# Five token blocks instead of seven in the first layer of an attention and feed-forward kernel

## The chip, the cores and the metric

The kernel runs on one core of a Trainium2 chip. Its metric is the device time of one execution in microseconds (us); the number told for a kernel is the median of its runs.

## What is computed

Attention over 4 batches, 8 heads, 576 positions and a head dimension of 64, with a mask that lets a position see 32 earlier ones: the last 32 for heads 0 to 3, and every fourth of the last 128 ("dilated") for heads 4 to 7. Its result, 2304 tokens of 512 features, goes through two layers with 2048 hidden features.

```python
scores = scale * np.matmul(q, k.transpose(0, 1, 3, 2))
scores = np.where(masks[None, :, :, :], scores, -1000000000.0)
attn = exp(scores - max) ; attn = attn / (attn.sum + 1e-09)
x = (attn @ v) as 2304 x 512
x = (h - tanh(h)) @ w_out,            h = x @ w_in       # layer one
out = (h * sigmoid(h)) @ w_out2,      h = x @ w_in2      # layer two
```

## The kernel before

**Features lie on the partitions.** `X` holds x^T: 4 groups of 128 features, each twice (a leading part in the short format `F32R`, and the rest, "hi" and "lo"), with 1152 columns, which is two batches of 576 tokens used in turn. Each product of the layers is made of three passes of TensorE (`passes`, L541): lo with hi, hi with hi, hi with lo.

**The layers run in token blocks.** `FIRST` lists those of layer one (seven, of 512, 304, 336, 272, 304, 272 and 304 tokens), and layer two has 4 of 512 and one of 256. In a block, 16 slots `f` each take 128 hidden features: `h` in 12 passes (4 feature groups of 3), the gate (tanh on ScalarE, a product or difference on VectorE, hi on ScalarE, lo on VectorE), and then the 12 passes of `y` for an earlier slot: one slot behind with blocks of more than `WIDE` tokens and in layer two, two behind with the small ones. Accumulators of `h` have two banks and those of `y` four.

**Weights are prepared on the chip.** A chunk (one slot of w_in or w_out) is loaded to a stage and goes through ScalarE three times (`prelu` L160, `lows` L165, `leading` L127), VectorE twice (`shift` L170, `trailing` L183) and GpSimd once (`join` L174). Layer one has 32 chunks. Those of layer two (`Feed`) are taken into the weight tiles of layer one while its last blocks still run: `FEED2` says how many chunks a slot takes, by `f % 3`.

**Attention runs in pairs of heads**, 16 of them. Batch 0 is done before layer one can start, by units of 192 positions: masked scores on TensorE, a maximum on VectorE, three exponentials on ScalarE, a division, a transpose on TensorE, the product with v, and the results into `X`. Batch 1 lies between the passes of block 0. All of that, with the weights of layer one and block 0 itself, is put in order by `play`, a planner with a cost for each step and due times (`SLOT0`, `SLOT`, `DUE`, `NEXT0`, `NEXT`); each engine executes its list strictly in that order.

**Batches 2 and 3 lie between the slots of the later blocks**, by numbered ticks. `STARTS` gives the tick at which a pair begins, and `plan` its steps: transposes of q and k on VectorE, scores, masks, exponentials, the division, eight transposes of the probabilities on VectorE, the product with v. `ORDER` is the order of the steps of a slot: gate `g`, hi `G`, lo `L`, `Y` the passes of y, `t` one tick, `F` the weights of layer two.

`WARM` products at the very start have no result that is used.

Of the kernel before, what the change touches and what calls it, by code (L numbers as in the profile page):

```python
# [8 lines left out]
F32 = mybir.dt.float32  # L9
F32R = mybir.dt.float32r  # L10
# [15 lines left out]
DIL = 4  # L26
MASKED = -1e30
# [4 lines left out]
def tile_kernel(  # L32
# [59 lines left out]

    def play(ops, free):
# [4 lines left out]
        while todo:  # L98
# [11 lines left out]
            t, o = min((x for x in first[e] if x[0] <= t + NEAR), key=lambda x: x[1].rank)  # L110
            o.fn(ENGINE[e])
# [21 lines left out]
    class Chunk:  # L133


        def __init__(self, store, key, src, is_in):
            self.store, self.key, self.src, self.is_in = store, key, src, is_in

# [137 lines left out]
    nc.scalar.copy(out=mask[QB:], in_=half)  # L276
    mask_dil = [mask[:, UB * u:UB * (u + 1)] for u in range(NU)]
    mask_plain = [mask[:, 0::5]] + [mask[:, NB - 1:]] * (NU - 1)

    kT1 = cpool.tile([P, S], F32, name="kT")  # L280
# [4 lines left out]
    class Pair:  # L285
# [220 lines left out]
        def values(self, n0, n1, pool=None, tag="o"):  # L506
# [5 lines left out]
            x = X[:, :, :, S * (self.b % 2):S * (self.b % 2 + 1)]  # L512
            src = o.rearrange("p m c -> p (m c)")
            s0, s1 = QB * n0, QB * n1
            if self.dil:
                dst = [x[:, w, self.c, s0:s1] for w in range(2)]
            else:
                i0, i1 = s0 // DIL, s1 // DIL
                dst = [x[:, w, self.c, :].rearrange("p (r i) -> p i r", r=DIL)[:, i0:i1, :] for w in range(2)]
                src = src.rearrange("p (i r) -> p i r", r=DIL)  # L520
            self.left[n0] = dst, src

        def x_hi(self, engine, n0):
            dst, src = self.left[n0]
            copy(engine, dst[0], src)

        def x_lo(self, n0):
            dst, src = self.left.pop(n0)
            nc.vector.tensor_tensor(out=dst[1], in0=src, in1=dst[0].bitcast(F32), op=ALU.subtract)
# [13 lines left out]
    class First:  # L543


        def __init__(self, t0, n):
            self.t0, self.n, self.layer = t0, n, 0
            self.x = X[:, :, :, t0 % (2 * S):t0 % (2 * S) + n]

        def parts(self, c):  # L550
            return [self.x[:, a, c] for a in range(2)]

# [4 lines left out]
        def begin(self, f, c, h):  # L557
# [4 lines left out]
            passes(h, [w[:, a, c, :] for a in range(2)], self.parts(c), c == 0, c == NC - 1)  # L562
            return h

        def second(self, f, g, opool):
            for c in range(NC):
                self.second_part(f, c, g)
            if f == NF - 1:
                for a, dst in ((0, y1_hi), (1, y1_lo)):
                    nc.sync.dma_start(out=dst[:, :, self.t0:self.t0 + self.n].rearrange("c p t -> p c t"),  # L570
                                      in_=self.x[:, a].bitcast(F32))

        def second_part(self, f, c, g):
            w = wout[0, f]
            if c == 0 and f == 0:
                self.y = [ps_y.tile([P, 512], F32, tag=f"y{k}", name=f"y{k}")[:, :self.n] for k in range(NC)]
            if True:
                passes(self.y[c], [w[:, a, c * P:(c + 1) * P] for a in range(2)],
                       [g[:, a] for a in range(2)], f == 0, f == NF - 1)
                if f == NF - 1:  # L580
                    hi, lo = self.parts(c)
                    nc.scalar.activation(out=hi, in_=self.y[c], func=AF.Copy)
# [426 lines left out]
```

## Time and profile before

| | |
|---|---|
| time, median of 3 runs | 915.97 us (915.05 to 916.33) |
| profiled execution | 915.71 us, of which the span in the profile is 913.9 us |
| TensorE busy | 896.9 us (98%) |
| VectorE, ScalarE, GpSimd busy | 436.0, 398.0, 122.6 us |
| mean granted TensorE clock | 0.986 of full |

The span is the time from the first to the last instruction. A share that is an average over the span says little here, since the start, the later part of layer one and layer two have different limits.

### The profile page before, as it was taken

To read this page: it belongs to the slowest core of one execution; us is meant where nothing else is said; L and a number is where in the kernel's file an instruction comes from. 1 tells how busy PE (TensorE), PEld (TensorE's weight loads), DVE (VectorE), ACT (ScalarE), POOL (GpSimd) and SP (SyncE) were. 2 spreads that over 40 slices of the span, in tenths; PEclk is the share of its full clock that TensorE was granted. 3 is DMA by queue.
4 is the path that set the end of the run, shared out by engine and by line. 5 is a ranking of instruction groups with operands and counts; after the bars stand their busy time and mean duration, and the time that the engine had idled before them with its cause. 6 is when DMAs were issued, how large, how long until landed. Compare 5 with 4: busy or idle time off the path is not lost.

```text
span 913.9 us, 15235 instructions
## 1 busy us (share of the span) xinstructions
PE 896.9 (98%) x5998; PEld 782.8 (86%) x5998; DVE 436.0 (48%) x836; ACT 398.0 (44%) x969; POOL 122.6 (13%) x164
## 2 busy tenths in 40 slices
PE   7999999999999999999999999999999999999997
PEld 5677778999999999999999888888888888888896
DVE  2468887446756666433266666422222222222232
ACT  5689875334443334423266666432223222322322
POOL 8333553000010000000022222100000000000000
PEclk9599999999999999999999999999999999999999
DMA  9966335213223322024044564140004000200100
GB/s 232 281 153 167 98 96 117 93 28 82 49 50 58 97 35 69 20 70 147 1 141 139 186 214 139 46 136 3 1 1 139 0 1 1 93 0 1 32 15 24
DMA packets 122375, 74.39 MB, mean 81 GB/s; under 512 B 84896, under 2 KB 110528, under 8 KB 122304
## 3 DMA queue, kind: packets, MB, share of 16 engines
q1 hardware_dynamic: 121472, 72.57, 28.6%
q0 software_dynamic: 832, 0.85, 0.4%
q8 instruction: 47, 0.77, 0.4%
q14 instruction: 24, 0.20, 0.1%
HBM read 59.24 MB, written 14.16 MB: 80 GB/s over the span
## 4 chain that ended last, share of the span: by engine, by line
PE 85%; DVE 5%; ACT 4%; issue 2%; DMA 2%; SPq 2%; DVEq 0%; ACTq 0%
PE h L541 39%; PE y L541 39%; PE s L432 3%; PE o L510 2%; DMA st<-in_moe_w_in_dram 1%; ACT w L127 1%; ACT st L160 1%; DVE g L555 1%; DVE pT L492 1%; SPq L359 1%; PE y L432 1%; PE h L387 1%; ACT gg L969 1%; DVE w L183 1%; DVE st L170 1%
## 5 line engine op out<-in xcount | busy, mean ns | idle before, releaser
L541 PE MATMUL h<-x,w 128*128 128x512 f32 (+4 forms) x2304 | 439.5, 338 | 0.8
L541 PEld LDWEIGHTS h<-x,w 128*128 128x128 f32 x2304 | 365.6, 188 | 45.2 <-DVE g L555 2.5
L541 PE MATMUL y<-gg,w 128*128 128x304 f32 (+3 forms) x1344 | 226.8, 314 | 0.0
L541 PE MATMUL y<-w,gg 128*128 128x512 f32 x864 | 209.8, 390 | 0.4 <-ACT gg L969 0.4
L541 PEld LDWEIGHTS y<-gg,w 128*128 128x128 f32 x1344 | 197.6, 188 | 8.8 <-DVE gg L882 0.7
L541 PEld LDWEIGHTS y<-w,gg 128*128 128x128 f32 x864 | 160.8, 188 | 34.3 <-ACT gg L969 1.2
L969 ACT ACTIVATE gg<-g 128x512 fp32r<-128x512 f32 (+4 forms) x176 | 90.7, 515 | 134.5 <-DVE g L555 74.6
L604 DVE SCALAR_TENSOR_TENSOR g<-g,h 128x512 f32<-128x512 f32 (+1 forms) x80 | 50.7, 633 | 200.6 <-ACT g L603 200.6
L971 DVE TENSOR_TENSOR gg<-g,gg 128x512 fp32r<-128x512 f32 (+4 forms) x176 | 96.9, 550 | 102.4 <-ACT gg L969 99.3
L603 ACT ACTIVATE g<-h 128x512 f32<-128x512 f32 (+1 forms) x80 | 44.4, 555 | 201.9 <-PE h L541 201.7
L174 POOL TENSOR_TENSOR st<-st 128x512 int32<-128x512 int32 x64 | 67.3, 1053 | 211.8 <-ACT st L165 179.2
L554 ACT ACTIVATE g<-h 128x304 f32<-128x304 f32 (+2 forms) x96 | 40.2, 418 | 122.6 <-PE h L541 117.8
L555 DVE TENSOR_TENSOR g<-h,g 128x304 f32<-128x304 f32 (+2 forms) x96 | 44.6, 465 | 82.3 <-ACT g L554 81.9
L183 DVE TENSOR_TENSOR w<-st,w 128x512 fp32r<-128x512 f32 x58 | 53.9, 933 | 24.0 <-ACT w L127 23.8
L160 ACT ACTIVATE st<-st 128x512 f32<-128x512 f32 x64 | 43.0, 671 | 8.9 <-DMA st<-in_moe_w_out_dram 4.5
L492 DVE STREAM_TRANSPOSE pT<-prob 32x288 f32<-32x288 f32 x96 | 44.9, 468 | 1.5
L127 ACT ACTIVATE w<-st 128x512 fp32r<-128x512 f32 x64 | 42.4, 664 | 4.0 <-POOL st L174 3.4
L165 ACT ACTIVATE st<-st 128x512 int32<-128x512 uint32 x64 | 43.3, 677 | 0.0
L469 ACT ACTIVATE prob<-prob,nb 128x96 f32<-128x96 f32 x108 | 38.8, 364 | 0.2 <-DVE nb L456 0.2
L479 POOL TENSOR_TENSOR prob<-prob,sum 128x864 f32<-128x864 f32 (+1 forms) x17 | 20.1, 1182 | 114.7 <-DVE sum L475 114.7
L170 DVE TENSOR_SCALAR st<-st 128x512 uint32<-128x512 uint32 x64 | 28.6, 455 | 6.6 <-ACT st L160 4.9
L510 PEld LDWEIGHTS o<-pT,v 96*64 96x64 f32 x576 | 21.6, 146 | 11.8 <-issue 4.3
(61 smaller groups left out, 421.2 us busy)
## 6 DMA issues: line engine op xcount, KB each, us to landing
st<-in_moe_w_in_dram SPq DMA_DIRECT2D x64, 256.0 KB
st<-in_moe_w_out_dram SPq DMA_DIRECT2D x32, 512.0 KB
x<-y_hi SPq DMA_DIRECT2D x4, 1024.0 KB
x<-y_lo SPq DMA_DIRECT2D x4, 1024.0 KB
qin<-in_q_dram SPq DMA_DIRECT2D x48, 72.0 KB
kin<-in_k_dram SPq DMA_DIRECT2D x48, 72.0 KB
v<-in_v_dram SPq DMA_DIRECT2D x16, 192.0 KB
y_hi<-x SPq DMA_DIRECT2D x3, 608.0 KB
```

Of the source, the lines that this page charges most:

```text
L127: engine.activation(out=out, in_=in_, func=AF.Copy, scale=1.0 if scale is None else scale)
L160: engine.activation(out=high, in_=high, func=AF.Prelu, scale=2.0 ** -112, alpha=2.0 ** 32)
L165: engine.activation(out=low.bitcast(I32), in_=low, func=AF.Copy, scale=2.0 ** -29)
L174: engine.tensor_tensor(out=high, in0=high, in1=self.low.bitcast(I32), op=ALU.add)
L183: engine.tensor_tensor(out=self.flat[:, 1], in0=self.high.bitcast(F32), in1=self.flat[:, 0].bitcast(F32), op=ALU.subtract)
L492: nc.vector.transpose(out=pT[32 * kk:32 * kk + 32, :, j, 32 * i:32 * i + 32], in_=self.p[p0:p0 + 32, :, 32 * kk:32 * kk + 32],)
L541: nc.tensor.matmul(o, stat[a], mov[b], start=first and n == 0, stop=last and n == 2)
L555: nc.vector.tensor_tensor(out=g, in0=h, in1=g, op=ALU.subtract)
L603: nc.scalar.activation(out=g, in_=h, func=AF.Tanh, scale=0.5)
L604: nc.vector.scalar_tensor_tensor(out=g, in0=g, scalar=1.0, in1=h, op0=ALU.add, op1=ALU.mult)
L969: nc.scalar.activation(out=gg[:, 0], in_=g, func=AF.Copy)
L971: nc.vector.tensor_tensor(out=gg[:, 1], in0=g, in1=gg[:, 0].bitcast(F32), op=ALU.subtract)
```

## The change

- Layer one has five blocks, four of 512 tokens and one of 256. For that the columns of `X` are turned by 128 (`SHIFT`): token t stands in column (t + 128) mod 1152. The last block lies in two pieces, columns 1024 to 1151 and 0 to 127, and is read through a view of two runs of 128. Columns of batches 2 and 3 whose place is still in use wait in a tile `late` and are copied at two ticks (`LATE_AT`).
- A slot of a 512 block in layer one has two ticks (`w` before the passes of y, `t` behind them), `STARTS` is given anew, and `STEPS` spreads the steps of a pair over more ticks.
- The first five chunks of layer two have tiles of their own (`PLUS`), and `FEED2` begins a block earlier at a lower rate.
- `play` adds products without a used result (`idle`) to TensorE's list where its plan has a gap, and there are 18 instead of 14 at the start. The costs and due times of the planner change (`DUE` 13 to 6, `NEXT0` 41 to 60, `NEXT` 20 to 16).

```diff
+    def idle(us):
+
+        for n in range(int((us - IDLE_GAP) / IDLE_US) if lent else 0):
+            nc.tensor.matmul(lent[0][:, UB * KB:], one[BF16], spare, start=True, stop=True)
...
             t, o = min((x for x in first[e] if x[0] <= t + NEAR), key=lambda x: x[1].rank)
+            if e == "T":
+                idle(t - free[e] + (MORE_IDLE if t < 12.0 else 0.0))
...
-            self.w = w = wpool.tile(shape, F32R, tag="win" if self.is_in else "wout", name="w")
+            self.w = w = self.room or wpool.tile(shape, F32R, tag="win" if self.is_in else "wout", name="w")
...
+        def column(self, s):
+            return (S * self.b + s + SHIFT) % (2 * S)
+
+        def late_columns(self):
+
+            at = LATE[self.b - 2]
+            a, n = self.column(at), S - at
+            hi, lo = (X[:, w, :, a:a + n] for w in range(2))
+            copy(nc.scalar, hi, late[:, :, :n])
+            nc.vector.tensor_tensor(out=lo, in0=late[:, :, :n], in1=hi.bitcast(F32), op=ALU.subtract)
...
-            self.x = X[:, :, :, t0 % (2 * S):t0 % (2 * S) + n]
+            at = (t0 + SHIFT) % (2 * S)
+            self.whole = at + n <= 2 * S
+            if self.whole:
+                self.x = X[:, :, :, at:at + n]
+                self.rows = [(t0, at, n)]
+            else:
+
+                m = n // 2
+                assert at + m == 2 * S
+                self.x = X.rearrange("p w c (k t) -> p w c k t", t=m)[:, :, :, 0::2 * S // m - 1]
+                self.rows = [(t0 + m, 0, m), (t0, at, m)]
...
-    FIRST = ((0, 512), (512, 304), (816, 336), (1152, 272), (1424, 304), (1728, 272), (2000, 304))
-    WIDE = 336
+    FIRST = ((0, 512), (512, 512), (1024, 512), (1536, 512), (2048, 256))
+    WIDE = 256
...
-    ORDER = "gGLYtF"
+    ORDER = "gGLwYtF"
...
-    STARTS = ((42, 46, 50, 54), (61, 69, 76, 83))
+    STARTS = ((33, 40, 46, 52), (59, 66, 74, 81))
+
+    STEPS = (1, 3, 4, 7, 8, 11)
...
-    WARM = 14
+    WARM = 18
+
+    IDLE_GAP, IDLE_US = 0.3, 0.11
...
-    DUE = 13.0
-    NEXT0, NEXT = 41.0, 20.0
+    DUE = 6.0
+    NEXT0, NEXT = 60.0, 16.0
...
-    FEED2 = ((1, 1, 1), (1, 1, 2))
+    PLUS = 5
+    FEED2 = ((0, 0, 1), (1, 0, 1), (1, 1, 2))
...
-                elif step == "t":
+                elif step == "t" or step == "w" and blk.n > WIDE and t < NB1:
                     run(todo.get(tick, ()))
                     tick += 1
```

Three places in the engines' lists show what moves.

ScalarE in the startup, from the copy of the first unit's transposed probabilities (`pT`) on. `prob` are exponentials, `x` results into `X`, and `st` a weight chunk in its stage; L160 is `prelu` of the first chunk. Before:

```order
L127 ACTIVATE pT<-y_331 96x384
L469 ACTIVATE prob,sum<-y_339,nb 128x96 x3
L127 ACTIVATE x<-o 128x48x4
L127 ACTIVATE pT<-y_365 96x384
L160 ACTIVATE st_179<-st_179 128x512
L469 ACTIVATE prob,sum<-y_372,nb 128x96 x3
L127 ACTIVATE x<-o 128x48x4
L127 ACTIVATE pT<-y_419 96x384
```

ScalarE of the change, from the same copy on; L169 and L174 are the first two steps of the first chunk there:

```order
L135 ACTIVATE pT<-y_342 96x384
L481 ACTIVATE prob,sum<-y_325,nb 128x96 x3
L135 ACTIVATE x<-o 128x48
L135 ACTIVATE x<-o 128x48x3
L135 ACTIVATE pT<-y_376 96x384
...
L481 ACTIVATE prob,sum<-y_397,nb 128x96 x3
L135 ACTIVATE x<-o 128x48
L135 ACTIVATE x<-o 128x48x3
L135 ACTIVATE pT<-y_485 96x384
L169 ACTIVATE st_184<-st_184 128x512
L174 ACTIVATE st_184<-st_184 128x512
```

The first chunk's first step stood behind the copies of two units, ahead of the fourth set of exponentials; now it stands behind the copies of four units, and two more sets of exponentials are ahead of it.

TensorE towards the end of the startup: products with v (`o`), transposes of the probabilities (`y<-one,prob`), masked scores (`y<-mask,one`, `y<-kT,qT`). Before, with the first passes of `h` between them:

```order
L510 MATMUL o<-pT,v 64x64 x6
L501 MATMUL y_727<-one_95,prob 96x128 x3
L541 MATMUL h<-x,w 128x512 x3
L425 LDWEIGHTS one_100
L425 MATMUL y_740<-mask,one_100 128x288
L432 MATMUL y_740<-kT,qT 64x96 x6
```

The same place in the change, where L97 is a filling product:

```order
L522 MATMUL o<-pT,v 64x64 x6
L513 MATMUL y_723<-one_95,prob 96x128 x3
L97 LDWEIGHTS one_100
L97 MATMUL y_698<-mask,one_100 128x224
L437 LDWEIGHTS one_100
L437 MATMUL y_729<-mask,one_100 128x288
L444 MATMUL y_729<-kT,qT 64x96 x6
```

The change has 26 filling products: one here, one a unit earlier, and 11 and 13 ahead of the last two units' transposes. No pass of `h` comes ahead of the last transposes any more.

VectorE in a later block, around the transposes of q and k of a dilated pair (`qT`, `kT`). `g` and `gg` are the gate, `pT<-prob` the transposes of the previous pair's probabilities, `prob<-s,mask` and `nb` the mask and maximum of the next scores. Before, in the 272 block at token 1152:

```order
L492 STREAM_TRANSPOSE pT<-prob 32x9x32 x4
L416 STREAM_TRANSPOSE qT<-qin 128x144x4
L416 STREAM_TRANSPOSE kT<-kin 128x144x4
L555 TENSOR_TENSOR g<-h,g 128x272
L971 TENSOR_TENSOR gg<-g,gg 128x272
L529 TENSOR_TENSOR x<-o,x 128x96x4
L453 SCALAR_TENSOR_TENSOR prob<-s,mask 128x288
L456 TENSOR_REDUCE nb<-prob 128x3
```

A dilated pair in the change, in the 512 block at token 512:

```order
L428 STREAM_TRANSPOSE qT<-qin 128x144x4
L486 TENSOR_SCALAR sum<-sum 128x9
L487 RECIPROCAL sum<-sum 128x9
L428 STREAM_TRANSPOSE kT<-kin 128x144x4
L610 TENSOR_TENSOR g<-h,g 128x512
L1059 TENSOR_TENSOR gg<-g,gg 128x512
L504 STREAM_TRANSPOSE pT<-prob 32x9x32 x8
L465 SCALAR_TENSOR_TENSOR prob<-s,mask 128x288
L468 TENSOR_REDUCE nb<-prob 128x3
```

The transposes of q and k no longer follow four others directly and stand further ahead of the scores that need them; all eight transposes of the probabilities now stand in one run ahead of a mask.

## Rows read from the trace of the kernel before

**Rows 1.** The page, 40 equal slices: busy tenths of TensorE and VectorE, and TensorE's granted clock.

```profile
PE   7999999999999999999999999999999999999997
...
DVE  2468887446756666433266666422222222222232
...
PEclk9599999999999999999999999999999999999999
```

**Rows 2.** Windows: stretch, length, busy us (x count) of PE, PEld, DVE, ACT, POOL; clock; DMA share; GB/s.

```profile
20.00:24.00 4.00, 0.54 (x18) 0.39 (x14) 1.00 (x4) 2.26 (x10) 3.44 (x6) 1.00 1.10 331
24.00:48.00 24.00, 22.93 (x249) 17.49 (x249) 11.63 (x33) 15.91 (x57) 8.80 (x13) 0.52 1.00 285
...
60.00:100.00 40.00, 40.00 (x273) 30.28 (x273) 35.29 (x71) 37.69 (x92) 15.54 (x16) 1.00 0.68 170
```

**Rows 3.** Timeline 0 to 31: start, us, engine, line, operation, count [idle before it, its releaser].

```profile
1.47 4.57 PE L725 MATMUL y<-warm 128*128 128x512 bf16 x14 [1.47 <-DVE warm L721]
...
21.74 0.65 ACT L160 ACTIVATE st<-st 128x512 f32<-128x512 f32 x1 [3.75 <-DMA st<-in_moe_w_in_dram]
...
24.10 0.57 PE L510 MATMUL o<-pT,v 96*64 96x64 f32 x12 [3.56 <-ACT pT L127]
```

**Rows 4.** Timeline of PE, undisturbed stretches of each block size: first and last start.

```profile
174.39 1.81 PE L541 MATMUL h<-x,w 128*128 128x304 f32 x12
...
194.28 1.81 PE L541 MATMUL h<-x,w 128*128 128x304 f32 x12
...
274.17 2.03 PE L541 MATMUL h<-x,w 128*128 128x336 f32 x12
...
277.88 2.03 PE L541 MATMUL h<-x,w 128*128 128x336 f32 x12
...
422.36 1.66 PE L541 MATMUL h<-x,w 128*128 128x272 f32 x12
...
452.45 1.66 PE L541 MATMUL h<-x,w 128*128 128x272 f32 x12
...
528.95 2.88 PE L541 MATMUL h<-x,w 128*128 128x512 f32 x12
...
855.35 2.88 PE L541 MATMUL h<-x,w 128*128 128x512 f32 x12
...
867.79 1.60 PE L541 MATMUL h<-x,w 128*128 128x256 f32 x12
869.23 1.55 PE L541 MATMUL y<-w,gg 128*128 128x512 f32 x6
```

**Rows 5.** Timeline of PE, the two waits in the blocks with batch 3.

```profile
338.18 0.78 PE L432 MATMUL s<-kT,qT 64*64 64x32 f32 x16 [0.99 <-DVE kT L416]
...
365.59 0.78 PE L432 MATMUL s<-kT,qT 64*64 64x32 f32 x16 [1.07 <-DVE kT L416]
```

**Rows 6.** Timeline, end of the last block of layer one: h on PE, one round on VectorE.

```profile
488.50 1.88 PE L541 MATMUL h<-x,w 128*128 128x304 f32 x12
...
495.34 0.46 DVE L555 TENSOR_TENSOR g<-h,g 128x304 f32<-128x304 f32 x1
...
...
499.01 0.46 DVE L555 TENSOR_TENSOR g<-h,g 128x304 f32<-128x304 f32 x1
...
510.59 3.06 PE L541 MATMUL h<-x,w 128*128 128x512 f32 x12
```

**Rows 7.** Timeline, from block 0 to block 1: gate of slot 15, results, next passes.

```profile
157.91 0.63 ACT L127 ACTIVATE gg<-g 128x512 fp32r<-128x512 f32 x1 [0.82 <-DVE g L880]
158.57 0.69 DVE L882 TENSOR_TENSOR gg<-g,gg 128x512 fp32r<-128x512 f32 x1 [0.76 <-ACT gg L127]
...
161.17 2.73 DVE L583 TENSOR_TENSOR x<-y,x 128x512 fp32r<-128x512 f32 x4 [1.91 <-ACT x L582]
162.38 3.88 PE L541 MATMUL h<-x,w 128*128 128x304 f32 x24
```

**Rows 8.** The page, costliest groups: count | busy us, mean ns | idle before.

```profile
L492 DVE STREAM_TRANSPOSE pT<-prob 32x288 f32<-32x288 f32 x96 | 44.9, 468 | 1.5
```

More of the change, by code (lines that the diff above doesn't have):

```diff
@@ L26 @@
 DIL = 4
+SHIFT = 128
 MASKED = -1e30
@@ new lines, in values, with cut @@
+            out = [(self.columns(a, b), x) for a, b, x in parts]
+            if not self.dil:
+                a = self.column(0)
+                x = X[:, :, self.c, a:a + last].rearrange("p w (r i) -> p w i r", i=CLS)[:, :, i0:i1]
+                out.append(([x[:, w] for w in range(2)], src[:, :, :DIL - 1]))
+            self.left[n0] = out
+        def column(self, s):
+            return (S * self.b + s + SHIFT) % (2 * S)
+        def cut(self, a, b):
+            at = {1: 2 * S - self.column(0), 2: LATE[0], 3: LATE[1]}.get(self.b, S)
+            return [(x, y) for x, y in ((a, min(b, at)), (max(a, at), b)) if x < y]
@@ L523, in x_hi, with columns @@
+        def columns(self, a, b):
+            if self.b > 1 and a >= LATE[self.b - 2]:
+                a, b = a - LATE[self.b - 2], b - LATE[self.b - 2]
+                return (late[:, self.c, a:b],)
+            a, b = self.column(a), self.column(b - 1) + 1
+            return [X[:, w, self.c, a:b] for w in range(2)]
         def x_hi(self, engine, n0):
-            dst, src = self.left[n0]
-            copy(engine, dst[0], src)
+            for dst, src in self.left[n0]:
+                copy(engine, dst[0], src)
@@ L561, in begin @@
             w = win[0, f]
-            passes(h, [w[:, a, c, :] for a in range(2)], self.parts(c), c == 0, c == NC - 1)
+            passes(self.view(h), [w[:, a, c, :] for a in range(2)], self.parts(c), c == 0, c == NC - 1)
             return h
@@ L755, in tile_kernel @@
                         held = {}
[L756 removed]
+                        a = op({"T": 0.5 if p.dil else 0.58}, lambda e, p=p, w=which, h=half, held=held: held.update(m=p.transpose_pe(w, h)),
                                [got[p, which], *ring_h.take()], r - 2 + which * 0.1)
@@ L931, in tile_kernel @@
         for t, f in slots + [(len(blocks), 0)]:
-            if tick == ATTN_END:
+            if tick >= ATTN_END and opool is None and stage is None:
                 attn.close()
+                second_weights = chunks(1, w_in2, w_out2)
+                plus = ctx.enter_context(tc.tile_pool(name="plus", bufs=1))
+                for k, ch in enumerate(second_weights[:PLUS]):
+                    ch.room = plus.tile([P, 2, NC, P] if ch.is_in else [P, 2, DM], F32R, tag=f"w{k}", name="w")
                 stage = ExitStack()
@@ L957, in tile_kernel @@
                     run_second()
-                ggs = g_tile([P, lag + 1, 2, 512 if lag == 1 else WIDE], F32R, "gg")
-            gg = ggs[:, n % (lag + 1), :, :blk.n]
+                ggs = g_tile([P, 4 * 512], F32R, "gg")
+            if f == 0 and lag == 2:
+                assert n % 2 == 0
+                n = 0
+            w = 512 if lag == 1 else WIDE
+            gg = ggs[:, 2 * w * (n % (lag + 1)):2 * w * (n % (lag + 1) + 1)].rearrange("p (a t) -> p a t", a=2)[:, :, :blk.n]
             g = g1[:, :blk.n]
@@ L973, in tile_kernel @@
                     waiting.append((blk, f, gg))
-                elif step == "F" and t >= NB1 - 1 and not feed2.done():
-                    for _ in range(FEED2[t - NB1 + 1][f % 3]):
+                elif step == "F" and t >= NB1 - 2 and stage and not feed2.done():
+                    for _ in range(FEED2[t - NB1 + 2][f % 3]):
                         feed2.front()
```

83 lines of the change are left out of this document (51 added, 32 removed).

## The prediction

> **What bounds the kernel now.** I read the page first: TensorE is busy nine tenths or more in every slice but the first and the last, so whatever shortens its own list shortens the kernel. But in the second slice, 23 to 46 us, its granted clock is 0.5 of full [rows 1]. Busy says nothing there about the speed of the work.
>
> So I took the start apart by windows [rows 2]. From 20 to 24 us TensorE has 0.54 us of work; from 24 to 48 it is busy 22.93 of 24 us, at a clock of 0.52; from 60 to 100 it is busy all 40 us at full clock, and ScalarE 37.69 of them and VectorE 35.29. The reader is to see three stretches: a hole, a stretch at half speed, and one in which TensorE bounds with two other engines close behind.
>
> The timeline says what made the hole [rows 3]. ScalarE stands 3.75 us ahead of the first step of the first weight chunk, whose load lands only at 21.7 us. ScalarE works strictly in order, so the exponentials and the copies of pT queued behind that step wait too, and TensorE waits 3.56 us for a pT. When it starts again, at 24.1, the clock has fallen, and it stays at half for nearly all of the next 24 us, though TensorE is then hardly ever idle [rows 2].
>
> Behind the start I compared stretches of pure passes by block size [rows 4], and looked for waits of TensorE: two at the scores of batch 3 [rows 5] and a slow last part of the last block of layer one [rows 6].
>
> **The change, part by part.** The sum is made against the profiled execution, 915.7 us (span 913.9 and 1.8 around it); the median of the runs, 915.97, is 0.3 above.
>
> *Block sizes.* From first and last starts [rows 4], a slot's 24 passes (12 of h, 12 of y) take 326.40/60 = 5.44 us at 512 tokens, 19.89/6 = 3.315 at 304, 30.09/10 = 3.009 at 272, 3.71 at 336; 12 passes of 256 take 1.44, so 24 take 2.88. Seven blocks need 5.44 + 3 x 3.315 + 2 x 3.009 + 3.71 = 25.11 us a slot, five need 4 x 5.44 + 2.88 = 24.64. Over 16 slots: **-7.5 us**. The columns are the same, so this is what 768 fewer passes cost beyond their columns, about 10 ns each. The term stands as long as TensorE bounds in the new blocks; if it didn't, it would be 0.
>
> The Trainium skill (TensorE: Matmul & The Clock Gate, Back-to-back issue gap) gives a pass at full clock a fixed 2.5 ns on top of its columns. By that, 768 passes would be worth 1.9 us, an estimate from that page, and the time 5.6 us longer than mine. The slopes of this trace contradict it, and I go by the trace.
>
> *The startup.* The first chunk now stands behind two more sets of exponentials on ScalarE. ScalarE reached it at 21.74 - 3.75 = 18.0 us. A unit takes ScalarE some 1.7 us (an estimate: from 24 to 48 us it is busy 15.91 us [rows 2], of which 9 steps of chunks take 5.9 at 0.65 each [rows 3], and the other 10 us hold six sets of exponentials with their copies), so two units bring it to about 21.4, when the load is just there. So the hole of 3.56 us should go, and with it, if nothing else idles, the fall of the clock; the 22.93 us of work at half clock then take 11.5 us. Together 15.0 us at most. Against that:
> - Four more warm-up products: 4.57/14 = 0.33 us each at most [rows 3], 1.3 at most, nothing if TensorE waits for q anyway. I take 0.6.
> - 26 filling products of 224 columns: scaled by columns from the same row 0.14 us each, 3.7 in all if every one delays work, 0 if each lies in a wait. They stand where the plan expects waits, so I take 1.0.
> - ScalarE. The attention's 10 us still fit into a stretch of 11.5, but the chunk steps don't: they are put off. Where block 0 starts, about 7 steps and three sets of exponentials are owed compared with before, some 7 us, and in the 40 us after that ScalarE has only 2.3 us free [rows 2]. I let 3.4 us of the gain go there, between none (if due times leave it room) and 5.
>
> That leaves **-10.0 us**, between +5 (the clock falls all the same, and fillers and warm-up come on top) and -15.
>
> *Spread steps in the later blocks.* The two waits for kT, 0.99 and 1.07 us [rows 5], came of scores one tick behind both transposes. Now there are two or three ticks between them: **-2.1 us**, at worst 0.
>
> *Weights of layer two.* In the last block, with a chunk in each slot, VectorE's round takes 499.01 - 495.34 = 3.67 us: gate, then two ScalarE steps and `leading` for a chunk, then `trailing`, for which it waits, then the next gate [rows 6]. A slot of 304 takes 3.315, so the gate falls back 0.36 us a slot until TensorE waits: six slots from 488.50 to 510.59 take 22.09 us instead of 19.89. The new block of 256 has a slot of 2.88 us but chunks in two of three. Two such rounds and a short one (gate, hi and lo, some 1.3 us) are 8.6 us, three slots 8.64: a tie, and a lag of two slots absorbs the unevenness. **-2.2 us**, at worst 0. The five own tiles let the chunks begin while their places are in use; for that alone I count nothing, since leading never waited for a place.
>
> *A drain that is no longer covered.* At the end of block 0 the order is h of the next block's slot 0, 24 passes of y, then the results on ScalarE and VectorE, and only then that slot's gate. Before, two more slots of h lay ahead of the first y (3.88 us from 162.38). Now block 1 runs one slot behind, so there is one h of 2.72 us. VectorE's results end at 163.90, and then sub, hi and lo of 0.69, 0.63 and 0.69 us [rows 7], with some 0.1 us between engines, give about 166.3, against 165.1 for the h: **+1.2 us**, between 0.5 and 2.
>
> *One slot behind with attention between.* The blocks from 512 on ran two slots behind and now run one. A pair adds eight transposes of 0.468 us, 3.7 in all [rows 8], in one or two runs, and a slot gives VectorE 5.44 us for those and two gate steps. I see a mask queued behind such a run making the next scores wait half a microsecond now and then: **+1.0**, between 0 and 8 (1 us for each of 8 pairs, as in rows 5).
>
> The extra pieces of copies into X (cuts at the turned columns), the copies out of `late`, and the later loads of y1 are hidden by the passes: VectorE is 4 to 7 tenths busy in the slices with batches 2 and 3 [rows 1]. Uncovered they would be some 3 us. The block in two pieces I count like one of 256.
>
> Sum: -7.5 - 10.0 - 2.1 - 2.2 + 1.2 + 1.0 = -19.6, so 915.7 - 19.6 = **896 us**.
>
> **The rivals.**
> - *The clock falls all the same*, because the first chunk or a head's data still comes late, or TensorE idles between the attention and the first y. For it: the fillers stand only near the end of the plan, none where the hole was, and the DMA engines are full throughout (1.00 to 1.10 in rows 2). Against it: the first slice has TensorE busy 7 tenths and the clock at 9 or more [rows 1], so short gaps don't lower it. Then the start gives 1 us instead of 10: 905 us. Chance 0.15.
> - *The weights put off come due.* ScalarE's debt of 7 us is paid in full by TensorE, 5 us beyond what the sum has, with the clock full: 901 us. For it: 37.69 of 40 us busy; against it: attention of batch 1 is moved later as well. Chance 0.15.
> - *Slower.* One slot behind, each set of scores in blocks 1 to 3 waits for a mask behind a run of transposes. There are 24 sets; at the 1.07 us of rows 5 each that is 25.7 us, and without the 1.0 counted above 915.7 - 20.6 + 25.7 = 921 us. It decides from (20.6 + 1.8)/24 = 0.9 us a set on. For it: eight transposes in one run; against it: the whole run fits a slot. Chance 0.04.
> - *The fillers and due times do nothing, and only the blocks count*: 905 us again; it is the first rival with another cause, and shares its chance.
>
> **How the numbers follow.** My case, clock kept and TensorE bound from block 0 on, has 0.64; its own range is 889 (the start gives 15 and no score waits: 896 - 5 - 1, with 1 us left for the drain) to 900. The two rivals at 901 and 905 have 0.30, the slower one 0.04, and 0.02 is for anything that ends within 0.2% of before, which is about what a measurement of this kernel can tell from no change. The range 889 to 905 holds about 8 in 10: of the first rival the half above 905 is out, with the slower one and the tails of mine. Faster 0.94, same 0.02, slower 0.04.
>
> **What would show it.** Granted clock 1.0 from 24 to 48 us and the startup's last product with v by about 44 us; h of slot 0 complete at about 46. Starts 5.44 us apart in blocks 1 to 3 wherever no attention lies between, 2.88 in the last, without a slow tail. No wait above 0.5 us at scores. About 1 us of wait at the first y of block 1. It is wrong if a clock of 0.5 stands after 20 us, if TensorE waits for ScalarE or VectorE at the start of block 0 for more than 5 us in all, or if the 512 blocks of layer one have slots longer than 5.44 us and their attention.

## The result, and the profile after

The change makes the kernel faster: 903.05 us (median of 4 runs, 901.63 to 905.87) against 916.15 us (915.05 to 917.30); the ratio is 0.986, with a 95% interval of 0.983 to 0.989. That is 13.1 us where 19.6 were forecast: inside the range of 889 to 905, but above the likeliest case's own range, which ended at 900. The mean granted clock of the four runs was 0.994, 0.998, 1.000 and 0.998; the profiled one is that of 0.994, the longest (905.87 us, span 904.1). What follows is read from that execution, which is 9.8 us shorter than the profiled one of before (915.71). The run at full clock took 902.25 us.

The page's slices of the changed kernel, the busy tenths of TensorE and its granted clock, answer to [rows 1]; the clock still has a low digit in the second slice.

```profile
PE   8899999999999999999998999999999999999998
...
PEclk9799999999999999999999999999999999999999
```

The windows of the start (stretch, length, busy us and count of PE, PEld, DVE, ACT, POOL, then clock, DMA share, GB/s) answer to [rows 2]:

```profile
20.00:24.00 4.00, 4.00 (x93) 3.29 (x89) 3.37 (x14) 2.89 (x15) 3.72 (x7) 1.00 1.06 328
24.00:30.00 6.00, 4.96 (x104) 4.01 (x105) 3.74 (x14) 4.56 (x20) 3.41 (x7) 0.98 1.06 326
30.00:36.00 6.00, 6.00 (x60) 4.69 (x60) 3.23 (x12) 2.48 (x12) 2.85 (x4) 0.50 1.06 356
36.00:42.00 6.00, 6.00 (x72) 4.45 (x70) 2.59 (x10) 4.11 (x18) 1.42 (x3) 0.67 0.97 235
```

From 20 to 24 us TensorE is busy all 4.00 us, where it was busy 0.54: the hole is gone. But the clock falls all the same, later and for less long, from 29.5 to 40 us instead of 24.5 to 49. The timeline of TensorE (start, us, operation, count, in brackets the idle time before it and its releaser) shows what came before that, and the marks of the start:

```profile
1.47 6.20 PE L799 MATMUL y<-warm 128*128 128x512 bf16 x18 [1.47 <-DVE warm L795]
7.60 1.21 PE L408 MATMUL h<-one,qin 96*64 96x96 f32 x24
...
28.06 0.22 PE L399 MATMUL h<-one,qin 72*64 72x72 f32 x1 [1.04 <-issue]
...
56.12 1.53 PE L583 MATMUL y<-gg,w 128*128 128x512 f32 x6
...
150.86 3.02 PE L583 MATMUL h<-x,w 128*128 128x512 f32 x12
...
502.95 2.91 PE L583 MATMUL h<-x,w 128*128 128x512 f32 x12
```

The clock fell after a pause of 1.04 us for which the profile names no releaser ("issue"), in the middle of a group of 16 transposes. The last three lines are marks: the first y of block 0 (64.11 before), the first h of block 1 and the first h of layer two. Before, the first h of block 1 stood here, and the first h of layer two at 510.59 [rows 6]:

```profile
155.29 1.82 PE L541 MATMUL h<-x,w 128*128 128x304 f32 x12
```

So the span divides into three, and the saving with it:

| stretch of the span | before | after | difference | forecast |
|---|---|---|---|---|
| start and block 0, to the first h of block 1 | 155.29 | 150.86 | -4.4 | -10.0 |
| later blocks, to the first h of layer two | 355.30 | 352.09 | -3.2 | |
| layer two and the end | 403.31 | 401.15 | -2.2 | |
| the last two together | | | -5.4 | -9.6 |

In the later blocks the slots are what the sum says. The timeline of undisturbed stretches, first and last start, answers to [rows 4]: 21.76/4 = 5.44 us a slot of 512, and 14.39/5 = 2.88 a slot of 256.

```profile
425.06 2.88 PE L583 MATMUL h<-x,w 128*128 128x512 f32 x12
...
446.82 2.88 PE L583 MATMUL h<-x,w 128*128 128x512 f32 x12
...
462.30 1.60 PE L583 MATMUL h<-x,w 128*128 128x256 f32 x12
...
476.69 1.60 PE L583 MATMUL h<-x,w 128*128 128x256 f32 x12
```

What is new behind block 0 are waits of TensorE, from the same timeline; the kernel before had those of [rows 5]:

```profile
162.77 3.01 PE L583 MATMUL y<-gg,w 128*128 128x512 f32 x12 [0.74 <-DVE gg L1059]
215.14 0.71 PE L444 MATMUL s<-kT,qT 64*64 64x96 f32 x12 [0.67 <-DVE prob L465]
236.44 0.71 PE L444 MATMUL s<-kT,qT 64*64 64x96 f32 x12 [0.68 <-DVE prob L465]
329.28 0.78 PE L444 MATMUL s<-kT,qT 64*64 64x32 f32 x16 [0.50 <-DVE kT L428]
460.04 2.41 PE L583 MATMUL y<-gg,w 128*128 128x256 f32 x12 [0.57 <-DVE x L641]
481.90 1.70 PE L583 MATMUL h<-x,w 128*128 128x256 f32 x12 [2.17 <-DVE g L610]
```

The last is the largest. VectorE's gate is late there because ScalarE, strictly in order, stands ahead of a chunk of layer two that hasn't landed. The timeline of SP's queue, and of ScalarE:

```profile
460.75 0.37 SPq L626 DMA_DIRECT2D y_hi<-x  x1
461.81 0.37 SPq L626 DMA_DIRECT2D y_lo<-x  x1
465.41 0.34 SPq L155 DMA_DIRECT2D st<-in_moe_w_out_dram  x1
465.80 1.25 SPq L656 DMA_DIRECT2D x<-y_hi  x1
469.33 0.36 SPq L656 DMA_DIRECT2D x<-y_lo  x1
469.79 1.36 SPq L153 DMA_DIRECT2D st<-in_moe_w_in_dram  x2
474.47 0.34 SPq L155 DMA_DIRECT2D st<-in_moe_w_out_dram  x1
...
478.58 0.68 ACT L169 ACTIVATE st<-st 128x512 f32<-128x512 f32 x1 [3.36 <-DMA st<-in_moe_w_in_dram]
```

Two stores of 1 MB of block 3's results, two loads of 1 MB for the first block of layer two, and chunks of 0.5 MB are issued within 14 us on the queue that moves all of them; the two chunk transfers issued at 469.79 are used only at 478.58, 3.36 us after ScalarE was ready for them.

### The profile page after: what moved, and what is told of

It is laid out like the page before. It is cut to its first block, busy times and chain, and to the rows that moved or that the text cites. A ratio compares the mean times of both kernels' runs of the same rounds, so it can differ in the third digit from the quotient of the medians.

```text
span 904.1 us, 13656 instructions
## 1 busy us (share of the span) xinstructions
PE 887.0 (98%) x5260; PEld 726.9 (80%) x5260; DVE 423.2 (47%) x782; ACT 386.5 (43%) x927; POOL 130.2 (14%) x168
## 4 chain that ended last, share of the span: by engine, by line
PE 74%; DVE 4%; ACT 2%; DMA 1%; issue 1%; ACTq 0%; DVEq 0%; SPq 0%
PE y L583 36%; PE h L583 35%; PE s L444 2%; PE o L522 1%; DVE pT L504 1%; DVE w L192 1%; DMA st<-in_moe_w_in_dram 1%; DVE g L610 1%; ACT w L135 1%; ACT gg L1057 1%; ACT st L169 0%; DVE gg L1059 0%; DVE st L179 0%; ACT g L609 0%; DVE x L641 0%
## 5 line engine op out<-in xcount | busy, mean ns | idle before, releaser
L583 PE MATMUL h<-x,w 128*128 128x512 f32 (+1 forms) x1920 | 428.3, 370 | 2.5 <-DVE g L610 2.2
L583 PEld LDWEIGHTS h<-x,w 128*128 128x128 f32 x1920 | 335.6, 188 | 65.7 <-DVE g L610 3.1
L583 PE MATMUL y<-gg,w 128*128 128x512 f32 (+1 forms) x960 | 219.4, 372 | 1.3 <-DVE gg L1059 0.7
L583 PEld LDWEIGHTS y<-gg,w 128*128 128x128 f32 x960 | 166.3, 188 | 34.4 <-DVE x L641 1.3
L1057 ACT ACTIVATE gg<-g 128x512 fp32r<-128x512 f32 (+1 forms) x144 | 84.2, 585 | 123.1 <-DVE g L610 63.1
L1059 DVE TENSOR_TENSOR gg<-g,gg 128x512 fp32r<-128x512 f32 (+1 forms) x144 | 91.2, 633 | 93.8 <-ACT gg L1057 89.5
L664 ACT ACTIVATE g<-h 128x512 f32<-128x512 f32 (+1 forms) x80 | 44.3, 554 | 196.9 <-PE h L583 196.9
L609 ACT ACTIVATE g<-h 128x512 f32<-128x512 f32 (+1 forms) x64 | 34.7, 543 | 131.5 <-PE h L583 125.7
L610 DVE TENSOR_TENSOR g<-h,g 128x512 f32<-128x512 f32 (+1 forms) x64 | 39.7, 620 | 90.0 <-ACT g L609 89.9
L192 DVE TENSOR_TENSOR w<-st,w 128x512 fp32r<-128x512 f32 x53 | 50.8, 962 | 25.7 <-ACT w L135 25.7
L169 ACT ACTIVATE st<-st 128x512 f32<-128x512 f32 x64 | 43.1, 673 | 7.6 <-DMA st<-in_moe_w_in_dram 5.0
L174 ACT ACTIVATE st<-st 128x512 int32<-128x512 uint32 x64 | 43.3, 676 | 0.0
L491 POOL TENSOR_TENSOR prob<-prob,sum 128x864 f32<-128x864 f32 (+1 forms) x15 | 17.8, 1185 | 87.3 <-DVE sum L487 82.7
```

The lines of the kernel that those rows point to most:

```text
L169: engine.activation(out=high, in_=high, func=AF.Prelu, scale=2.0 ** -112, alpha=2.0 ** 32)
L174: engine.activation(out=low.bitcast(I32), in_=low, func=AF.Copy, scale=2.0 ** -29)
L192: engine.tensor_tensor(out=self.flat[:, 1], in0=self.high.bitcast(F32), in1=self.flat[:, 0].bitcast(F32), op=ALU.subtract)
L583: nc.tensor.matmul(o, stat[a], mov[b], start=first and n == 0, stop=last and n == 2)
L610: nc.vector.tensor_tensor(out=g, in0=h, in1=g, op=ALU.subtract)
L664: nc.scalar.activation(out=g, in_=h, func=AF.Tanh, scale=0.5)
```

## The experiments

**The two halves apart.** The first kernel is the kernel before with the edits of the startup, the second the changed kernel without them (the planner's costs and `MORE_OUT` go with these lines).

```diff
-    WARM = 14
+    WARM = 18
-    DUE = 13.0
-    NEXT0, NEXT = 41.0, 20.0
+    DUE = 6.0
+    NEXT0, NEXT = 60.0, 16.0
+            if e == "T":
+                idle(t - free[e] + (MORE_IDLE if t < 12.0 else 0.0))
...
```

> The kernel before with only the edits of the startup: due times, planner costs, 18 warm-up products, filling products; blocks, turned columns and feed of layer two stay as before. First theory (the two halves of the change add, and the start is the larger): the hole at 20 us is gone, and the gain is 4.4 us where the clock still falls for 10 us and up to 9 where it doesn't: 907 to 912 us. Rival (the start's gain needs the new blocks, since the weights put off come due in block 0 and delay it): under 2 us gained, 914 or more, with waits of TensorE between 60 and 160 us.

> The changed kernel with the startup of before: due times, costs, 14 warm-up products, no filling products. First theory: blocks 1 to 4 and the step into layer two gain 4.7 us, 911 to 912, with the same waits in them as in the changed kernel (0.7 at the first y of block 1, three of 0.5 to 0.7 at scores, 2.2 in the last block), and the start as in rows 3 of before. Rival (the waits in the later blocks come of work that the new startup puts off): they are gone, and the gain is 7.5 to 9, 907 to 908.

Measured: the start alone 908.08 us (907.04 to 909.44) against 916.31, ratio 0.991 (0.990 to 0.992), so 8.2 us; the blocks alone 911.50 (910.25 to 912.07), ratio 0.994 (0.993 to 0.996), 4.8 us. Together 13.0, and the whole change gives 13.1: the halves add, to within what the runs of each kernel differ by, and both first theories hold. In the profile of the start alone the clock never fell, and block 1 begins at 147.20, 8.1 us earlier than before:

```profile
7.84 1.21 PE L405 MATMUL h<-one,qin 96*64 96x96 f32 x24
...
28.08 0.22 PE L396 MATMUL h<-one,qin 72*64 72x72 f32 x1 [0.61 <-issue]
...
147.20 1.92 PE L550 MATMUL h<-x,w 128*128 128x304 f32 x12
```

In that of the blocks alone the waits of the later blocks are all there, up to 2.42 us for the late chunk, so they don't come of the new startup. The start's shortfall is thus some 2 us without a fall of the clock, and that of the later blocks some 5 us.

**Filling products out.**

```diff
-        for n in range(int((us - IDLE_GAP) / IDLE_US) if lent else 0):
+        for n in range(0):
```

> The changed kernel without its 26 filling products. First theory (they lie in waits of TensorE, and the clock is up by then anyway): no difference, 902 to 904, the clock stays full from 42 us on. Rival one (they keep the clock up through the waits at 43 to 48 us): without them it falls again at about 47, the first passes of h run at half, and the time is 4 to 10 us longer. Rival two (they delay the transposes behind them): 2 to 3 us shorter, about 900.

Measured: 901.70 us (899.83 to 903.68), ratio 0.984 (0.982 to 0.985); beside the changed kernel's 903.05 (901.63 to 905.87) that is not told apart from no difference. In the profile TensorE has two waits at the end of the startup, and behind them the clock is at half:

```profile
39.38 0.53 PE L513 MATMUL y<-one,prob 128*96 128x128 f32 x3 [1.10 <-POOL prob L491]
41.11 0.53 PE L513 MATMUL y<-one,prob 128*96 128x128 f32 x3 [1.20 <-POOL prob L491]
41.58 0.92 PE L522 MATMUL o<-pT,v 96*64 96x64 f32 x24
...
42.00:48.00 6.00, 6.00 (x41) 4.40 (x36) 2.24 (x6) 3.68 (x9) 3.11 (x3) 0.53 0.56 100
```

That is what rival one said of the clock, without the time it gave. The stretch itself is shorter: the products with v come 3.83 us behind the transposes at 37.75, where the changed kernel takes 5.17 (42.64 to 47.81). So the filling products cost 1.3 us there: the first of them waits 1.59 us for ScalarE, because the bank that they write in is still being read by exponentials. The mean clock of the five runs is 0.991 to 0.997, with a median of 0.996; the four of the changed kernel have 0.994 to 1.000, with a median of 0.998. One profile couldn't say how the two balance, so the question was put again below.

**The first load of layer two taken apart.**

```diff
-            if (t, f) == (NB1 - 1, LAG + 1):
-                blocks[NB1].load()
+            if t == NB1 - 1 and f in (6, 10):
+                blocks[NB1].load_part(f > 6)
```

> The changed kernel with the load of the first block of layer two (y1, two transfers of 1 MB at slot 3 of the last block of layer one) taken apart: leading parts at slot 6, the rest at slot 10. First theory (the 2.2 us wait of TensorE at 481.9 comes of a weight chunk whose load lands late behind these two transfers): the wait is gone or under 0.5 us, 2 us shorter. Rival (with three stages a chunk is late wherever the transfers lie): the wait moves to a slot behind 6 or 10 and the time stays; if y1 lands too late, layer two starts up to 2 us later.

Measured: 900.23 us (899.80 to 901.13), ratio 0.983 (0.981 to 0.984): 2.8 us less than the changed kernel. The wait is gone, and every slot of the last block takes 2.88 us:

```profile
460.19 1.59 PE L583 MATMUL h<-x,w 128*128 128x256 f32 x12
...
494.74 1.60 PE L583 MATMUL h<-x,w 128*128 128x256 f32 x12
497.62 2.68 PE L583 MATMUL h<-x,w 128*128 128x512 f32 x11
```

Twelve slots take 34.55 us. From the first single h of the last block to layer two it is 41.86 us (455.76 to 497.62) and was 45.07 (457.88 to 502.95), so the place of this load cost 3.2 us in the profile, the 2.17 and small delays besides. This profile had the clock at half from 11 to 22 us; the last wait of TensorE ahead of that was 1.08 us, ending at 10.76.

The next four start from this kernel.

**Fourteen warm-up products** (`WARM = 18` to 14).

> The run with y1 taken apart (900.2 us), and 14 instead of 18 warm-up products. First theory (each warm-up product delays the first transposes of q, since q is there by 6 us): the first transposes start 1.3 to 1.9 us earlier and all of it reaches the end: 898.3 to 899. Rival one (the loads of later heads bound the start): the first transposes are earlier, the first pass of h isn't, and the time stays at 900. Rival two (the four products keep the clock up): the clock falls longer or more often, 901 to 904.

Measured: 897.07 us (896.58 to 897.88), ratio 0.979 (0.9774 to 0.9805): 3.2 us less than with 18, more than the first theory gave, and rivals one and two fail. In this profile the clock didn't fall, and the four runs have a mean clock of 0.998 to 1.000, where the kernel that it started from had 0.994 to 0.998; so the 3.2 us may hold some of that too.

**Filling products in an early wait.**

```diff
         def transpose_pe(self, which, half):
+            if (self.c, which, half) == (1, 0, 0):
+                for n in range(9):
+                    nc.tensor.matmul(lent[0][:, UB * KB:], one[BF16], spare, start=True, stop=True)
```

> The run with y1 taken apart, and nine more filling products ahead of the second pair's transposes of q, where TensorE waits 1.08 us for a copy of kT. First theory (it is this wait after which the clock fell at 11 us in two of the profiles): the clock stays full from 8 to 21 us, and the time is the same or up to 1 us shorter, since the transposes behind wait anyway. Rival (the fall comes with something else, the warm-up's end or a moment of the chip's own): a stretch at half clock before 21 us all the same, and up to 0.5 us longer for the fillers.

Measured: 900.13 us (897.56 to 900.27; the profiled run is the 897.56), ratio 0.982 (0.980 to 0.983). Its clock stayed full throughout; three of the four runs took the time of the kernel without these products. No difference of the median. The wait of 1.08 us is gone, and neither here nor in the version below that has these products does the clock fall before 21 us; of the ten profiles with that wait three have such a fall. That fits the first theory, but two profiles are too few to show it.

**Two pairs a tick earlier** (`STARTS` 33, 40 to 32, 39).

> The run with y1 taken apart, with the first two pairs of batch 2 one tick earlier (32 and 39 for 33 and 40), so that the second pair's last transposes and the third's first scores no longer share a tick. First theory (a mask behind a run of transposes makes the next scores wait 0.68 us, once for each such shared tick): one of the two waits for masks in block 1 goes, the other stays, 0.5 to 0.8 us shorter. Rival (one slot behind, a mask is late wherever transposes stand near): both waits stay or move, no difference.

Measured: 898.46 us (897.87 to 902.89), ratio 0.981 (0.979 to 0.983). One of the two waits for a mask went and the other stayed, as the first theory has it:

```profile
232.30 0.71 PE L444 MATMUL s<-kT,qT 64*64 64x96 f32 x12 [0.68 <-DVE prob L465]
```

The median is 1.8 us below that of the kernel it started from, but its runs spread over 5 us, so only the 0.68 is shown.

**A block of 512 in two of 256.**

```diff
-    FIRST = (..., (1536, 512), (2048, 256))
+    FIRST = (..., (1536, 256), (1792, 256), (2048, 256))
-    FEED2 = ((0, 0, 1), (1, 0, 1), (1, 1, 2))
+    FEED2 = ((0, 0, 1), (0, 0, 0), (1, 0, 1), (1, 1, 2))
```

The first gate of the second block of 256 is written where the last gate of the block ahead is still to be read, so the products of one slot take other numbers; operations and sizes are as planned.

> The run with y1 taken apart, with the fourth block of 512 (token 1536) in two of 256, at the same ticks: 384 more passes with the same columns; the feed of layer two takes two chunks fewer before the last block. First theory (a pass costs some 10 to 13 ns beyond its columns, from 5.44 us a slot against two of 2.88): 16 x 0.32 = 5.1 us longer, and 0.6 more for one more step between blocks: 905 to 906.5. By the 2.5 ns that the Trainium skill (TensorE: Matmul & The Clock Gate, Back-to-back issue gap) gives a pass beyond its columns, 1.0 us and the step: 901.5 to 902.

Measured: 905.63 us (903.81 to 907.60), ratio 0.988 (0.986 to 0.989), 5.4 us more than with the block whole. The timeline shows 27 slots of 256 in a row, 77.75/27 = 2.88 us each, and no wait of TensorE between them:

```profile
371.54 1.60 PE L583 MATMUL h<-x,w 128*128 128x256 f32 x12
...
449.29 1.60 PE L583 MATMUL h<-x,w 128*128 128x256 f32 x12
```

So 384 more passes cost 16 x (2 x 2.88 - 5.44) = 5.1 us by the slots, 13 ns each; the medians differ by 5.4, with one more step between blocks in it. The 2.5 ns of the Trainium skill (TensorE: Matmul & The Clock Gate, Back-to-back issue gap) would make 1.0 us of the 384 passes, an estimate from that page. The Trainium skill states them there for an isolated product, and says that in a stream with weight loads both together set the spacing. Here every pass has a weight load of its own, and the measured 13 ns decide.

**Versions that put these together**, all with y1 taken apart and the pairs earlier: 14 warm-up products; 10; 14 with the early filling products; 14 without the 26 filling products.

> The run with y1 taken apart, with both 14 warm-up products and the earlier pairs: if the two act in different places they add, 897.1 - 0.7 = 896.4 us, with one wait for a mask left in block 1. If the 1.8 us of the earlier pairs alone were more than the wait of 0.68 that went, 895.3.

> As the run with both (14 warm-up products, earlier pairs), with 10 warm-up products. First theory (each product delays the start by 0.3 us, since q lies there): the first transposes start at about 5.3 us or wait for q, and the time is 1 us shorter. Rival (the products bring the clock or the engine's pace up in time): the transposes and products of the start are slower than 0.72 us for 12 or the clock falls, and the time is the same or longer.

> As the run with both, with nine filling products ahead of the second pair's transposes of q, where a wait of 1.08 us stood ahead of a fall of the clock at 11 us in two profiles. If that wait is what lets the clock fall there: no fall before 21 us, the single times lie closer together, and the median is 0 to 0.5 us shorter. If not: 0.4 us longer, since they end 0.4 us behind the copy they wait beside.

> As the run with both, without the 26 filling products of the plan. In the profile without them the stretch from the transposes of the third last unit to the last two units' products with v took 3.83 us (37.75 to 41.58), with them 5.17 (42.64 to 47.81): first theory, they cost 1.3 us where the clock is full, and don't keep it up (it fell behind them in two profiles): 1.3 us shorter. Rival (they keep the clock up more often than not): the clock falls behind that stretch in more of the runs, and the time is the same or up to 2 us longer.

Measured: 897.90 (896.40 to 899.36), 896.12 (895.88 to 901.64), 897.66 (895.60 to 902.18) and 898.00 us (897.03 to 898.41), with ratios of 0.980, 0.979, 0.980 and 0.980 and intervals of 0.977 to 0.982 around them. None is told apart from another, nor from 897.07 with 14 products alone: the gain of the earlier pairs did not show in the time a second time, and four products fewer gave only 0.6 us there (898.46 to 897.90). Neither the filling products nor their absence show in the time. In the profiles the end of the startup reads as before: with the filling products 42.48 - 37.31 = 5.17 us, without them 43.02 - 39.20 = 3.82.

```profile
39.43 1.21 PE L97 MATMUL y<-mask,one 128*128 128x224 bf16 x11 [1.59 <-ACT prob L481]
...
42.48 0.92 PE L522 MATMUL o<-pT,v 96*64 96x64 f32 x24
```

```profile
42.56 0.54 PE L513 MATMUL y<-one,prob 128*96 128x128 f32 x3 [1.20 <-POOL prob L491]
43.02 0.92 PE L522 MATMUL o<-pT,v 96*64 96x64 f32 x24
```

(The first of these two is the version with both edits, the second the one without filling products.) The latter began its first transposes 0.43 us later and had its clock at half from 31 to 34.5 us, which can hide the 1.3 us in this profile. The mean clocks of the runs say more: 0.998, 0.996, 0.996 and 0.996 without the filling products, 0.999, 0.998, 0.998 and 0.998 with them. The medians differ by 0.002, as with the changed kernel above, and 0.002 of 895 us is 3.6 us at half clock, or up to 1.8 us of work. So the rival fits better than the first theory: the filling products cost 1.3 us, keep the clock up longer, and the two about cancel. With four and five runs on a side that is likely and not certain. Ten warm-up products give three of the fastest runs (895.9 to 896.1) and one of the slowest (901.64); in the profile of that one the products take 4.45 us, the next 24 transposes 1.99 instead of 1.21, and the clock is at half from 11 to 21.5:

```profile
1.47 4.45 PE L804 MATMUL y<-warm 128*128 128x512 bf16 x10 [1.47 <-DVE warm L800]
5.85 1.99 PE L408 MATMUL h<-one,qin 96*64 96x96 f32 x24
```

The fourteen products without further edits are the version to keep: 6.0 us less than the changed kernel and 19.7 less than before, with a spread of 1.3 us.

## Why the prediction came out as it did

The mechanisms named are mostly there, and two terms of the sum were too large: that of the start by 2 us and more, by what the clock does in the run, and those of the later blocks by 4 to 5. The likeliest case missed by its own bounds. The result lies in the range because the range also took in the times of the rivals at 901 and 905, and neither of these came as described: the clock fell, but later and for less long than in the first, and little of ScalarE's debt was paid as the second has it. (The low end of the range, 889, is one less than its terms give: 896 - 5 - 1 = 890.)

**The hole** went, as the step says, and the first chunk no longer holds ScalarE up.

**The fall of the clock** did not go with it, and a clock of 0.5 after 20 us was one of the prediction's own signs of being wrong. The prediction argued that short gaps don't lower the clock and gave 0.15 to a fall all the same. The profiles of the twelve kernels with the new startup speak against the argument. The table lists for each the start of the first transposes of q, the stretches at half clock (1.2 GHz) before 55 us, the last wait of TensorE ahead of the fall, and the first h of block 1:

| kernel | first q, us | clock at half, us | wait ahead of it, us | first h of block 1, us |
|---|---|---|---|---|
| 14 products | 6.55 | none | | 144.92 |
| both edits | 6.91 | none | | 145.49 |
| early filling products | 7.01 | none | | 145.98 |
| both edits, no filling products | 7.34 | 31.0 to 34.5 | 1.13, to 30.78 | 146.03 |
| both edits, early filling products | 6.54 | 39.5 to 43.0 | 1.59, to 39.03 | 146.74 |
| start alone | 7.84 | none | | 147.20 |
| earlier pairs | 7.71 | 40.0 to 43.5 | 1.59, to 39.64 | 147.35 |
| no filling products | 7.10 | 11.5 to 15.0 and 42.0 to 49.5 | 1.08, to 10.89; 1.20, to 41.11 | 147.95 |
| y1 taken apart | 6.96 | 11.0 to 22.0 | 1.08, to 10.76 | 148.71 |
| 10 products | 5.85 | 11.0 to 21.5 | 1.08, to 10.42 | 149.75 |
| the change | 7.60 | 29.5 to 40.0 | 1.04, to 28.06 | 150.86 |
| block in two | 7.78 | 30.0 to 37.0 and 43.5 to 47.5 | 1.31, to 28.52; 1.59, to 43.72 | 151.52 |

In eight of twelve the clock falls, each time within 2 us of the end of a wait of 1.0 to 1.6 us; in the other four it doesn't, though they have waits of the same kind and length at the same places. The plainest case stands elsewhere, in the version without filling products: in the last block of layer one, where passes had followed one another without a gap for some 17 us, a single wait of 1.79 us is followed by the clock at half from 479.3 to 482.8.

```profile
478.69 2.46 PE L583 MATMUL h<-x,w 128*128 128x256 f32 x12 [1.79 <-DVE g L610]
...
479.50:482.50 3.00, 3.00 (x16) 3.00 (x16) 1.34 (x4) 2.37 (x5) 0.31 (x1) 0.50 0.53 174
```

At the same place the changed kernel waits 2.17 us, and the blocks alone 2.42, and there the clock stays full. So one such wait can be enough, and whether it is differs from execution to execution; what decides it, no run here shows. The mean clocks of all runs say how often the new startup gets through. The four profiles without a fall read 0.999 or 1.000, and so do 13 of the 43 runs with filling products and none of the 9 without. It matters: in the version with ten products the two runs at 1.000 took 895.88 and 896.11 us, and the one at 0.993 901.64. Where the fall lies makes no clear difference. From the first q to the first h of block 1, falls of 10.5 to 11 us cost 2.4 to 5.5 us at 11 us and 3.9 to 4.9 at 29.5, against the profiles without one. The filling products help without securing it: the clock fell right behind the eleven and thirteen in three of the ten profiles that have them, and behind the end of the startup in one of the two that haven't.

**With a clock that stays up** the start gives 8.1 to 10.4 us (the four rows with none, from 155.29), and with fourteen products and a fall of 3.5 us 8.6 and 9.3: the step's 10.0 was the case of a clock that stays up and a short warm-up. The startup's last product with v, forecast for about 44 us, starts at 43.56 to 45.90 in these four, and at 49.56 in the changed kernel. There the start gave 4.4, and by the windows some 5.1 us of work were lost to the half clock (0.50 of 6 us, 0.33 of 6 and 0.02 of 6).

**Warm-up.** Four more products were put at 0.6 us; the first transposes began 1.6 us later in the profile (5.98 before, 7.60 after). That is the upper bound of the step, 1.3, and more, because products did not all take the 0.33 us of the row that it went by. But the first transposes start anywhere from 6.54 to 7.34 us in the four new versions with fourteen products and from 6.96 to 7.84 in the seven with eighteen, so one profile of each doesn't give the price. The two pairs of versions that differ in these products alone have medians 3.2 us (900.23 and 897.07) and 0.6 us (898.46 and 897.90) apart, so the size is not settled. From first q to the first h of block 1 the profiles without a fall have 138.4 to 139.4 us, whatever the warm-up: a later start goes through whole.

**The weights put off** were put at 3.4 us, and between the first y and the first h of block 1 the changed kernel takes 94.74 us instead of 91.18, which is 3.6. The smaller part of it is the mechanism that was named. The windows of the two stretches, first before and then after:

```profile
64.11:155.29 91.18, 91.00 (x596) 70.52 (x594) 77.56 (x146) 73.81 (x173) 40.72 (x43) 1.00 0.52 122
56.12:150.86 94.74, 93.44 (x626) 72.57 (x624) 81.16 (x162) 80.62 (x199) 51.70 (x49) 1.00 0.53 134
```

TensorE has 2.4 us more work there and 1.1 more idle time. The work is what had filled the waits of the startup: before, 30 passes of h and three sets of scores of batch 1 lay ahead of the first y, now 24 and one, and these have to be done later (by the rows some 1.4 us for six passes and 0.7 for each set). The idle time is one wait of 1.21 us at the end, and that does come of a late weight chunk: on VectorE the result that TensorE waits for stands behind the last step of a chunk, which waits for ScalarE, which waits for GpSimd.

```profile
148.32 0.69 ACT L135 ACTIVATE w<-st 128x512 fp32r<-128x512 f32 x1 [1.46 <-POOL st L183]
149.05 0.79 DVE L192 TENSOR_TENSOR w<-st,w 128x512 fp32r<-128x512 f32 x1 [1.06 <-ACT w L135]
...
150.36 0.57 PE L522 MATMUL o<-pT,v 96*64 96x64 f32 x12 [1.21 <-DVE x L563]
```

The size was right by luck, for two thirds of it have another cause.

**Block sizes**: right. The slots are 5.44 and 2.88 us, and the block taken in two gives 13 ns for a pass, where the sum had 10 over its mix of sizes.

**Slow tail** of the last block: the tie of 8.64 us for three slots and two rounds of VectorE holds, as the slots of 2.88 show once y1 is out of the way. What the sum lacked is the transfers: it counted the chunks' time on VectorE and called the later loads of y1 hidden, without adding up what SP's queue carries in that block. The load at slot 3 came right behind 2 MB of stores, and put 3.2 us back. That is the largest single error in the later blocks.

**Waits.** The kT waits were 2.06 us and should have gone; 0.50 is left. One slot behind was put at 1.0; the two waits for masks are 1.35, and where the runs of transposes and the scores share no tick there is none, so the slower rival, a wait at each of 24 sets, was never near. The drain of block 0 was put at 1.2 and took 0.74; a second one of the same kind, at the step from 512 to 256, took 0.57 and was not in the sum. Together 3.16 instead of 2.2.

**The later blocks add up** to this: forecast -9.6; with the 3.2 of the load -6.4; with 1.0 more of waits -5.4, which is what was measured. It closes better than it should: the step into layer two and the end gave 2.2 us that the forecast hadn't (1.45 in its first three slots and 0.70 behind the last product), and so some 2 us more were lost among the passes that stand beside attention. No run here takes these apart, and it stays open.

## What to carry to other kernels

Removing the longest wait of a start does not keep TensorE's clock up: a fall can follow a wait of a microsecond too, so price both cases and look at several executions before a gain is put down to the clock. When loads are moved, add up what their queue carries in that stretch, stores and other loads with it; a load for later work that stands right behind a store of results can hold up the small transfers that the next slots need. And work that had filled waits is not free once the waits are gone: count it where it lands.

## What the runs showed of the hardware

TensorE's pace in the warm-up about doubles at a moment that differs by 2 us and more from execution to execution, while the granted clock reads 1.00 all along. Of the 512-column products, the kernel before started 7 between 4.5 and 5.5 us, and the version with both edits and without filling products 4 there and 3 in the next:

```profile
4.50:5.50 1.00, 1.00 (x7) 0.44 (x5) 0.00 (x0) 0.00 (x0) 1.00 (x4) 1.00 1.04 203
```

```profile
4.50:5.50 1.00, 1.00 (x4) 0.39 (x3) 0.00 (x0) 0.00 (x0) 1.00 (x4) 1.00 1.11 204
5.50:6.50 1.00, 1.00 (x3) 0.30 (x2) 0.00 (x0) 0.00 (x0) 1.00 (x6) 1.00 1.01 208
```

Fourteen products took from 4.57 to 5.93 us for that reason. The Trainium skill (TensorE: Matmul & The Clock Gate, What you observe) has this moment differ by half a microsecond either way between runs; the traces agree that it moves, and show it moving further.

The pause without a releaser stood at the same instruction in three profiles (28.06, 28.08 and 28.52 us, 0.61 to 1.31 us long), eight TensorE products later in the version with eight fewer ahead of it (31.62 us, 1.31), and not at all in the others. A fixed place in the list of instructions, while the DMA engines are full, speaks for instructions that arrive late; no run took that apart.
